# Rewriting the order table of a fused gated-attention and MLP kernel on one Trainium2 core

## The chip, the core and the metric

The kernel runs on one core of a Trainium2 chip (trn2). Its time is the device time of that core in microseconds (us); several runs are taken and their median is compared. The engines are TensorE (PE: matmuls, and beside them its weight loads, PEld), VectorE (DVE), ScalarE (ACT), GpSimd (POOL) and SyncE (SP, which here issues nearly all DMAs).

## The reference

Two parts, the second fed by the first. In float32, with 4 batches, 8 heads, 768 tokens, head size 48:

```python
f = 1.0 / (1.0 + np.exp(-f_logit))
for t in range(S):                                # 768 tokens
    state = f[:, :, t, :, None] * state + k_t (x) v_t     # per head, 48 x 48
    y[:, :, t] = q_t @ state
x = y.transpose(0, 2, 1, 3).reshape(3072, 384)
h = x @ w_in                                      # 384 x 2048
g = h * np.clip(h + 3.0, 0.0, 6.0) / 6.0
out = g @ w_out                                   # 2048 x 384
```

## The kernel before

**Units.** The attention runs in chunks: 24 units of 128 tokens (chunk 0 of the four batches is units 0 to 3, chunk 1 units 4 to 7, and so on). A unit takes these steps, each called by a token name and the unit's number. SP loads `load` (the gates' logits, L308, two buffers), `loadq` (q and k, L312, a ring of three) and `loadv` (v, L317, a ring of three). `gate` is the sigmoid on ACT (L321). DVE makes running products of the gates: `back` (a scan, L327), `rend` (L343 and L344) and `fwd` (a second scan, L347). `kmul` (L340), `qmul` (L353) and `decay` (L356) scale k, q and the carried state; they run on DVE, or on GpSimd if the list ON_POOL names them. TensorE then does `tk` (transposes of k, L411), `kv` (the new state, L430), `att` (the products of q and k, L392, 32 small matmuls), `qs` (q times the old state, L461) and `av` (L478). Between them `ktok` (ACT, L418) copies the transposed k, `mask` (DVE, L399) applies the causal mask to what `att` left in PSUM, `carry0` and `carry1` (L443 to L452) update the state, `xh` (ACT, L497) and `xl` (DVE, L500) write the result as a float16 high and low part, and `hole` (SP, two DMAs at L507) copies some rows of it.

**Weights.** Both weight matrices come in 16 blocks of 128 of the 2048 hidden columns. Block f is loaded by `ld` (SP, `raw`, 768 KB, two buffers, L233) and turned into a float16 high and low part by `z` (ACT, L238), `cy` (ACT, L247), `mid`, `lim`, `dif`, `top` (DVE, L251, L257, L263, L267), `high` (ACT, L272) and `low` or its halves `lowi` and `lowo` (L275, DVE or GpSimd).

**MLP.** The tokens form six groups of 512, one for each chunk. A step is one group with one block; steps are numbered 16 times the group plus the block, 0 to 95. A step is `mm1` (9 float16 matmuls of 128x512, L526), `relu` (ACT, L536), `g` (DVE, L540), `gh` (ACT, L545), `gl` (DVE or GpSimd, L550 and L555) and `mm2` (9 matmuls, L572). For blocks 0 to 4 of group 0 the first matrix product is done in halves of 256 tokens as soon as two units are there: `mm1a`/`mm1b` (L593), `relua`/`relub` (L602), `ga`/`gb` (L606), `mm2a`/`mm2b` (float32, L611); blocks 5 to 7 use `mm2x` (L583). In the last group `mm2` is split into `mm2m0`, `mm2m1` (L572) and the halves `mm2p`, `mm2q` (L626). `outv` (DVE) or `outs` (ACT) reads a finished bank and `od`, `odh` write it out; in the tail `outh` does half of one.

**The checks.** `wtop`, `xtop`, `xsum`, `xleast`, `flag0`, `finite`, `count` and last `judge` (DVE, L725 to L728) reduce the inputs' sizes to one flag. At the end all five engines load the flag and branch (L820) past a general version of the kernel that is not needed for these inputs.

**Warm-ups.** `warm.N` puts N bf16 matmuls of 128x512 on a blank tile (L794) into TensorE's row; nothing reads them.

**What sets the order.** The table ORDER is one long string of tokens `op.number`, with PSUM banks behind a second dot where a step needs them. The program emits the steps in this sequence and ties every instruction to the one before it on its engine, so each engine, and SP's DMA queue, works strictly in the table's order, and waits whenever its next instruction isn't ready. There is no scheduler behind it. A step may change engines only between DVE and GpSimd, by the list ON_POOL, or by its name (`outv`/`outs`). The loop that emits the steps follows.

Of the kernel before, what the change touches and what calls it, by code (L numbers as in the profile page):

```python
# [58 lines left out]
loadv.3 kv.3.0 carry0.3 warm.1 qs.3.2 av.3 loadq.4 carry1.3 xh.2 ld.2 top.1 high.1 mm2a.0 kmul.4 rend.4 xl.2 xh.3 xl.3
lowi.1 fwd.4 mm1a.1.4 z.2 cy.2 mid.2 carry1.2 tk.4.0 ktok.4 qmul.4 lim.2 load.5 relua.1 loadv.4 kv.4.2 ga.1 gate.5  # L60
ld.3 z.3 att.4.2 hole.2 mm2a.1 hole.3 dif.2 top.2 back.5 cy.3 mid.3 loadq.5 kmul.5 decay.4 carry0.4 high.2 mm1b.0.0
relub.0 gb.0 mm1b.1.4 tk.5.1 lowi.2 mm1b.2.0 relub.1 gb.1 lim.3 rend.5 mm1a.2.4 relub.2 mm2b.0 dif.3 fwd.5 top.3 gb.2
mm2b.1 relua.2 loadv.5 ld.4 load.6 ga.2 ld.5 z.4 cy.4 loadq.6 load.7 mm2b.2 carry1.4 mid.4 decay.5 high.3 lim.4 gate.6
lowi.3 mm1a.3.4 dif.4 back.6 top.4 z.5 ktok.5 relua.3 mm1b.3.0 relub.3 high.4 ga.3 kmul.6 mm2a.2 qmul.5 lowi.4 gb.3
mask.4 rend.6 cy.5 mid.5 fwd.6 mm2a.3 lim.5 mm1a.4.0 relua.4 ga.4 ld.6 mm1b.4.4 z.6 gate.7 dif.5 mm2b.3 tk.6.0 ktok.6
relub.4 mm2a.4 loadv.6 qmul.6 top.5 back.7 cy.6 mid.6 att.5.0 qs.4.2 high.5 decay.6 kv.6.0 load.8 gate.8 lowi.5 av.4
xh.4 gb.4 ld.7 mm1.5.4 carry0.6 carry1.6 lim.6 dif.6 loadq.7 mm2b.4 z.7 xl.4 top.6 kv.5.2 relu.5 ld.8 g.5 mm2x.5
mask.5 cy.7 kmul.7 mid.7 loadv.7 tk.7.0 carry0.5 lim.7 hole.4 rend.7 dif.7 high.6 lowi.6 mm1.6.4 z.8 top.7 cy.8 qs.5.2
# [875 lines left out]
```

## Time and profile before

| | |
|---|---|
| median of three runs (489.01, 490.39, 491.16) | 490.39 us |
| the profiled execution | 489.08 us |
| its span in the trace | 487.4 us |
| its mean granted TensorE clock | 0.982 |
| busy PE / weight loads | 464.9 / 248.0 us |
| busy DVE / ACT / POOL | 305.5 / 201.8 / 99.2 us |
| moved by DMA | 40.78 MB, 84 GB/s |
| of it by the instruction queue q8 | 41 transfers, 0.67 MB |

How to read it: the span is the time from the first to the last record; 1.7 us lie outside of it. In a timeline each row is a run of like instructions: its start in us, the time it was busy, the engine, the line, output and inputs, the shape, and how many; in brackets the idle time of the engine ahead of it and what ended that ("issue" means that the engine waited for nothing that the profile shows). In a table of stretches each row has the stretch and its length, the busy time and count of PE, PEld, DVE, ACT and POOL, the clock that TensorE was granted (1.00 is full speed), the share of the 16 DMA engines and the GB/s. In groups of instructions the busy sum and the mean in ns of one come first, then the idle time ahead of them. In the DMA rows stand the count, the size of one and the median time from issue to landing.

### The profile page before, as it was taken

To read this page: it belongs to the slowest core of one execution; us is meant where nothing else is said; L and a number is where in the kernel's file an instruction comes from. 1 tells how busy PE (TensorE), PEld (TensorE's weight loads), DVE (VectorE), ACT (ScalarE), POOL (GpSimd) and SP (SyncE) were. 2 spreads that over 40 slices of the span, in tenths; PEclk is the share of its full clock that TensorE was granted. 3 is DMA by queue.
4 is the path that set the end of the run, shared out by engine and by line. 5 is a ranking of instruction groups with operands and counts; after the bars stand their busy time and mean duration, and the time that the engine had idled before them with its cause. 6 is when DMAs were issued, how large, how long until landed. Compare 5 with 4: busy or idle time off the path is not lost.

```text
span 487.4 us, 11581 instructions
## 1 busy us (share of the span) xinstructions
PE 464.9 (95%) x4980; PEld 248.0 (51%) x4980; DVE 305.5 (63%) x519; ACT 201.8 (41%) x336; POOL 99.2 (20%) x97
## 2 busy tenths in 40 slices
...
GB/s 230 132 294 113 233 171 232 152 152 208 22 93 1 81 50 132 2 196 22 1 66 9 76 77 1 83 152 139 37 43 1 0 1 4 67 0 1 0 1 71
DMA packets 24553, 40.78 MB, mean 84 GB/s; under 512 B 2480, under 2 KB 17072, under 8 KB 24496
## 3 DMA queue, kind: packets, MB, share of 16 engines
...
q8 instruction: 41, 0.67, 0.6%
...
## 4 chain that ended last, share of the span: by engine, by line
PE 77%; DVE 11%; DMA 5%; issue 3%; ACT 2%; POOL 0%; SPq 0%; DVEq 0%; POOLq 0%; ACTq 0%
PE o L572 30%; PE pair L526 22%; PE single L526 9%; DMA qkf<-qk 3%; PE pair L392 2%; PE pair L461 2%; PE o L611 2%; PE pair L478 2%; PE pair L430 2%; DVE tg L540 2%; DMA raw<-w 1%; DVE weight L275 1%; PE single L626 1%; PE pair L626 1%; DVE suffix L327 1%
## 5 line engine op out<-in xcount | busy, mean ns | idle before, releaser
L572 PE MATMUL o<-gg,weight 128*128 128x512 f16 x744 | 170.8, 379 | 3.4 <-ACT gg L545 3.1
L526 PE MATMUL pair<-xts,weight 128*128 128x512 f16 x585 | 133.6, 379 | 0.0
L526 PEld LDWEIGHTS <-weight 128*128 128x128 f16 x819 | 79.0, 98 | 94.4 <-issue 1.6
L572 PEld LDWEIGHTS <-weight 128*128 128x128 f16 x744 | 71.7, 98 | 87.1 <-issue 5.6
L545 ACT ACTIVATE gg<-tg 128x512 f16<-128x512 f32 x88 | 55.0, 628 | 82.2 <-DVE tg L540 50.4
L555 POOL TENSOR_TENSOR gg<-tg,gg 128x512 f16<-128x512 f32 x38 | 47.6, 1254 | 172.0 <-ACT gg L545 157.8
L540 DVE SCALAR_TENSOR_TENSOR tg<-tg,pair 128x512 f32<-128x512 f32 x65 | 43.8, 682 | 53.2 <-ACT tg L536 53.2
L536 ACT ACTIVATE tg<-pair,half 128x512 f32<-128x512 f32 x65 | 44.2, 683 | 77.5 <-PE pair L526 68.7
L526 PE MATMUL single<-xts,weight 128*128 128x512 f16 x234 | 54.8, 379 | 0.0
L555 DVE TENSOR_TENSOR gg<-tg,gg 128x512 f16<-128x512 f32 x34 | 24.7, 731 | 28.7 <-ACT gg L545 28.3
L540 DVE SCALAR_TENSOR_TENSOR tg<-tg,single 128x512 f32<-128x512 f32 x26 | 17.7, 682 | 24.2 <-ACT tg L536 23.0
L347 DVE TENSOR_TENSOR_SCAN suffix<-gates,rend 112x516 f32<-112x516 f32 x24 | 30.5, 1270 | 3.1 <-POOL qkf L340 2.2
L327 DVE TENSOR_TENSOR_SCAN suffix<-gates,unit 112x516 f32<-112x516 f32 x24 | 29.4, 1223 | 2.9 <-ACT gates L321 2.8
L399 DVE TENSOR_TENSOR a<-pair,causal 128x512 f32<-128x512 f32 x24 | 16.4, 684 | 17.7 <-PE pair L478 10.0
L536 ACT ACTIVATE tg<-single,half 128x512 f32<-128x512 f32 x26 | 17.7, 682 | 22.6 <-PE single L526 22.2
L340 POOL TENSOR_TENSOR qkf<-qkf,suffix 112x512 f32<-112x512 f32 x13 | 16.4, 1264 | 48.4 <-DVE suffix L327 34.5
L500 DVE SCALAR_TENSOR_TENSOR xts<-pair,xts 112x512 f16<-112x512 f32 x24 | 16.4, 685 | 12.9 <-ACT xts L497 12.5
L353 POOL TENSOR_TENSOR qkf<-qkf,suffix 112x512 f32<-112x512 f32 x11 | 15.0, 1361 | 44.0 <-PE pair L392 27.3
L497 ACT ACTIVATE xts<-pair 112x512 f16<-112x512 f32 x24 | 14.2, 593 | 21.5 <-PE pair L478 19.0
L392 PE MATMUL pair<-qkf 48*64 48x64 f32 x768 | 17.2, 223 | 5.7 <-issue 5.6
L275 POOL TENSOR_TENSOR weight<-whole,weight 128x384 f16<-128x384 f32 (+1 forms) x10 | 10.6, 1059 | 39.4 <-ACT weight L272 39.4
L392 PEld LDWEIGHTS pair<-qkf 48*64 48x64 f32 x768 | 14.3, 136 | 7.5 <-issue 6.3
...
## 6 DMA issues: line engine op xcount, KB each, us to landing
raw<-w SPq DMA_DIRECT2D x16, 768.0 KB, 4.9
qkf<-qk SPq DMA_DIRECT2D x24, 448.0 KB, 4.6
gates<-fg SPq DMA_DIRECT2D x24, 226.2 KB, 3.2
v<-v SPq DMA_DIRECT2D x24, 200.0 KB, 4.3
...
```

The lines of the kernel that those rows point to most:

```text
L327: nc.vector.tensor_tensor_scan(flat(sf)[:, ::-1], gt[:, 1:][:, ::-1], flat(unit)[:, ::-1], 0.0, op0=ALU.mult, op1=ALU.add,)
L340: engine("kmul", i).tensor_tensor(parts_of(t, 1), parts_of(t, 1), split(sf[:, :, 1:C + 1]), op=ALU.mult)
L347: nc.vector.tensor_tensor_scan(flat(sf), gt[:, :NP * (C + 1)], flat(rend), 0.0, op0=ALU.mult, op1=ALU.add,)
L392: nc.tensor.matmul(d["at"][HC * odd:HC * (odd + 1), e, 2 * n + c], t[rs, 1, n, c, odd], t[rs, 0, n, c, odd], start=True, stop=True,)
L399: nc.vector.tensor_tensor(d["a"].rearrange("r p e t -> r e p t"), d["at"], causal.unsqueeze(1).unsqueeze(1).broadcast_to([128, 2, NP, HC]) ...
L500: nc.vector.scalar_tensor_tensor(parts(1), d["y"][:PR], 2.0 ** XBITS, parts(0), op0=ALU.mult, op1=ALU.subtract)
L526: nc.tensor.matmul(h, win[:, f, a, k * 128:(k + 1) * 128], g["xt"][:, k, :g["n"] // C, b], start=i == 0, stop=i == 3 * KT - 1,)
L536: nc.scalar.activation(d["t"], d["h"], AF.Relu, bias=half, scale=RISE)
L540: nc.vector.scalar_tensor_tensor(d["t"], d["t"], TOP, d["h"], op0=ALU.min, op1=ALU.mult)
L545: nc.scalar.activation(d["gg"][:, 0], d["t"], AF.Copy)
L555: engine("gl", int(g["name"]) * NF + f).tensor_tensor(d["gg"][:, 1], d["t"], d["gg"][:, 0], op=ALU.subtract)
L572: nc.tensor.matmul(g["o"][m], wout[:, f, a, m * 128:(m + 1) * 128], g[f]["gg"][:, b], start=f == 0 and i == 0, stop=f == NF - 1 and i == 2 ...
```

## The change

The string ORDER is written anew: the same steps, 1389 tokens for 1386, in another sequence from the first line to the last. Apart from that:

- ON_POOL has 77 names for 82. kmul.13, kmul.18, qmul.11, gl.17, gl.19, gl.21, gl.35, gl.52, gl.64, gl.67, gl.69 and lowo.4 go from GpSimd to DVE; decay.14, decay.16, qmul.10, gl.45, gl.72, gl.74 and lowo.2 go from DVE to GpSimd. Of the output copies outv.2 becomes outs.2, outv.14 becomes outs.14, and outs.4 becomes outv.4.
- The warm-ups at the start are 16, 2, 3, 4, 4, 3, 5, 6, 2, 2, 1 matmuls; before they were 16, 2, 3, 2, 2, 6, 12, 3, 2, 1. That is 48 for 49.
- The branch at the end carries a hint for the engines' instruction fetch. Before, it named DVE, ACT, POOL and SP at mm1.94 and PE at mm2m1.95. Now it names ACT behind mm1.92 and PE ahead of mm2m1.95, and the other three no longer.
- In the tail `judge` stands behind outv.16, before it stood ahead of mm2p.94; in the list of late steps gl.81 now stands ahead of mm2p.81 and mm2q.81, and mm2.79 and mm1.82 stand between mm1.81 and them.

The diff, with a piece of the table and the code:

```diff
 ORDER = """
...
-mask.0 av.0 xh.0 ld.1 fwd.1 load.3 qmul.1 warm.2 kv.1.2 carry0.1 att.1.0 back.2 mask.1 rend.2 xl.0 z.0 cy.0 mid.0
...
+gate.2 qmul.1 back.2 ktok.1 ld.0 loadq.2 load.3 xh.0 cy.0 xl.0 rend.2 att.1.0 mask.1 warm.4 kv.1.2 z.0 mid.0 carry0.1
...
@@ -781,10 +781,7 @@
-    HINTS = {"mm1.94.2": [e for e in ORDERED if e != ENG.PE], "mm2m1.95": [ENG.PE]}
     for token in ORDER:
-        if token in HINTS:
-            tc.mark_branch_hint_location("general", "LikelyTaken", HINTS[token])
         settle()
         op, i, *tail = token.split(".")
         i = int(i)
@@ -795,6 +792,8 @@
+        elif op == "hint":
+            tc.mark_branch_hint_location("general", "LikelyTaken", [(ENG.PE, ENG.Activation)[i]])
         elif op in FLAG:
```

Three places of the order are needed below. Numbers behind an underscore only number the tiles. The first is SP's queue at the start, from the load of unit 2's q and k on: `gates` is a `load`, `qkf` a `loadq`, `v` a `loadv`, `raw` an `ld`, `xts` a `hole`. Before:

```order
L312 DMA qkf2_227<-qk 112x1024
L233 DMA raw1_256<-w 128x3072
L308 DMA gates1_77<-fg 112x517
L507 DMA xts_112<-xts_112 16x3x256 x4
L312 DMA qkf3_389<-qk 112x1024
L317 DMA v2_393<-v 128x400
L308 DMA gates0_75<-fg 112x517
L317 DMA v3_509<-v 128x400
L312 DMA qkf4_562<-qk 112x1024
L233 DMA raw2_566<-w 128x3072
```

And now:

```order
L312 DMA qkf2_260<-qk 112x1024
L308 DMA gates1_77<-fg 112x517
L317 DMA v2_351<-v 128x400
L233 DMA raw1_353<-w 128x3072
L312 DMA qkf3_357<-qk 112x1024
L507 DMA xts_112<-xts_112 16x3x256 x4
L317 DMA v3_454<-v 128x400
L308 DMA gates0_75<-fg 112x517
L312 DMA qkf4_512<-qk 112x1024
L233 DMA raw2_539<-w 128x3072
L317 DMA v4_541<-v 128x400
```

raw1 (ld.1) stood two places ahead of the rows copy and of unit 3's q and k; now gates1 of unit 3 and v2 stand ahead of it, and a `gates` load can go only when its buffer has been read by `fwd` of two units before. gates0, qkf4, raw2 and v4 now follow each other directly.

The second is DVE from `back` of unit 2 (L327) on; L399 is mask.1, the two rows of L500 are xl.0 (from pair1) and xl.1 (from pair0), L343 and L344 are rend.2, L347 is fwd.2, and L251 to L267 convert weight block 0. Before:

```order
L327 SCALAR_TENSOR_TENSOR suffix0_76<-gates0_75,unit_94 112x516
L399 TENSOR_TENSOR a1_305<-pair0_70,causal_84 128x2x4x64
L343 TENSOR_SCALAR ends_111<-suffix0_76 112x4
L344 RECIPROCAL rend_109<-ends_111 112x4
L500 SCALAR_TENSOR_TENSOR xts_112<-pair1_71,xts_112 112x4x128
L251 TENSOR_SCALAR raw0_225<-top0_311 128x768
L340 TENSOR_TENSOR qkf2_227<-qkf2_227,suffix0_76 112x512
L257 TENSOR_SCALAR top0_311<-top0_311 128x768
L500 SCALAR_TENSOR_TENSOR xts_112<-pair0_70,xts_112 112x4x128
L263 TENSOR_TENSOR top0_311<-top0_311,raw0_225 128x768
L267 SCALAR_TENSOR_TENSOR whole_73<-top0_311,whole_73 128x768
```

And now:

```order
L327 SCALAR_TENSOR_TENSOR suffix0_76<-gates0_75,unit_94 112x516
L500 SCALAR_TENSOR_TENSOR xts_112<-pair1_71,xts_112 112x4x128
L343 TENSOR_SCALAR ends_111<-suffix0_76 112x4
L344 RECIPROCAL rend_109<-ends_111 112x4
L399 TENSOR_TENSOR a1_285<-pair0_70,causal_84 128x2x4x64
L251 TENSOR_SCALAR raw0_258<-top0_264 128x768
L340 TENSOR_TENSOR qkf2_260<-qkf2_260,suffix0_76 112x512
L257 TENSOR_SCALAR top0_264<-top0_264 128x768
L347 SCALAR_TENSOR_TENSOR suffix0_76<-gates0_75,rend_109 112x516
L263 TENSOR_TENSOR top0_264<-top0_264,raw0_258 128x768
L500 SCALAR_TENSOR_TENSOR xts_112<-pair0_70,xts_112 112x4x128
L267 SCALAR_TENSOR_TENSOR whole_73<-top0_264,whole_73 128x768
```

mask.1 went from the place right behind `back` to behind rend.2, xl.0 from behind rend.2 to ahead of it, and fwd.2 and lim to dif of the weight block stand ahead of xl.1 now.

The third is TensorE around att.1 (L392). L430 is kv.1, L794 (in the new file L791) is a warm-up, L478 is av. Before, the last rows of kv.1 and then att.1:

```order
L430 MATMUL pair1_71<-v1_191,ktok1_234 64x48
L430 MATMUL pair1_71<-v1_191,ktok1_234 48x48
L392 MATMUL pair0_70<-qkf1_187 64x64 x16
L794 LDWEIGHTS blank_88
L794 MATMUL idle_124<-blank_88 128x512
```

And now, the end of av.0 and then att.1:

```order
L478 MATMUL pair1_71<-a0_218,v0_159 64x64 x8
L478 MATMUL pair1_71<-a0_218,v0_159 48x64 x8
L392 MATMUL pair0_70<-qkf1_189 64x64 x16
L791 LDWEIGHTS blank_88
L791 MATMUL idle_124<-blank_88 128x512
```

att.1 stood behind all of kv.1; now it comes right behind av.0 (and the four warm-ups and kv.1 come behind att.1). Further on, the table has mm1a.0 (nine matmuls of 128x256), kv.2, att.2, att.3 before, and now att.2, kv.2, mm1a.0, att.3.

More of the change, by code (lines that the diff above doesn't have):

```diff
@@ L59 @@
[L59 to L68, printed above, removed]
@@ L134 @@
[L134 to L138 removed]
+load.0 loadq.0 gate.0 load.1 back.0 rend.0 kmul.0 gate.1 warm.16 tk.0.1 ktok.0 fwd.0 back.1 loadv.0 warm.2 kv.0.2
```

169 lines of the change are left out of this document (89 added, 80 removed).

## Prediction

> **What bounds the kernel now.** I read the page's head first, then busy time by stage, then the timelines of TensorE (PE) and VectorE (DVE) over the first 62 us, the DMA view of short stretches, and the tail.
>
> ```profile
> span 487.4 us, 11581 instructions
> PE 464.9 (95%) x4980; PEld 248.0 (51%) x4980; DVE 305.5 (63%) x519; ACT 201.8 (41%) x336; POOL 99.2 (20%) x97
> q8 instruction: 41, 0.67, 0.6%
> 61.00:122.00 61.00, 58.38 (x765) 32.50 (x764) 58.91 (x100) 40.48 (x59) 15.15 (x13) 1.00 0.57 183
> 122.00:474.00 352.00, 349.54 (x3420) 177.90 (x3419) 198.30 (x324) 129.60 (x222) 76.33 (x64) 1.00 0.17 47
> ```
>
> The last two rows are stages: after the length, the busy time of PE, weight loads, DVE, ACT and POOL. From 122 to 474 us PE is busy 349.5 of 352 us. It is the bound; its matmuls are the same in both kernels, so an order can save only its 2.5 us of gaps there. From 61 to 122 us DVE is busy 58.9 of 61 us and PE 58.4: both are full. What an order can win lies before 61 us. PE there:
>
> ```profile
> 12.12 0.60 PE L794 MATMUL idle<-blank 128*128 128x512 bf16 x2
> 12.91 0.85 PE L430 MATMUL pair<-v,ktok 64*64 64x48 f32 x46 [0.18 <-ACT xts L497]
> 17.22 0.90 PE L392 MATMUL pair<-qkf 48*64 48x64 f32 x19 [3.16 <-issue]
> 35.41 0.46 PE L392 MATMUL pair<-qkf 48*64 48x64 f32 x16 [2.42 <-issue]
> 38.87 2.93 PE L611 MATMUL o<-th,whole 128*128 128x256 f32 x6
> 41.59 2.00 PE L593 MATMUL single<-xts,weight 128*128 128x256 f16 x9
> 45.69 1.56 PE L611 MATMUL o<-th,whole 128*128 128x256 f32 x6
> 47.09 1.15 PE L593 MATMUL pair<-xts,weight 128*128 128x256 f16 x9
> ```
>
> Twice PE stops inside a block of attention matmuls and waits for nothing that the profile shows ("issue"): 3.16 us in att.1, 2.42 us in att.3. DVE works on unit after unit in a fixed order, and its largest waits answer to these:
>
> ```profile
> 12.62 0.69 DVE L353 TENSOR_TENSOR qkf<-qkf,suffix 112x512 f32<-112x512 f32 x1
> 18.16 0.69 DVE L399 TENSOR_TENSOR a<-pair,causal 128x512 f32<-128x512 f32 x1 [3.70 <-PE pair L392]
> 21.64 0.69 DVE L500 SCALAR_TENSOR_TENSOR xts<-pair,xts 112x512 f16<-112x512 f32 x1 [0.79 <-ACT xts L497]
> 35.94 0.69 DVE L399 TENSOR_TENSOR a<-pair,causal 128x512 f32<-128x512 f32 x1 [2.78 <-PE pair L392]
> 44.95 0.42 DVE L606 SCALAR_TENSOR_TENSOR th<-th,single 128x256 f32<-128x256 f32 x1 [2.36 <-ACT th L602]
> ```
>
> mask.1 waits 3.70 us for att.1, mask.3 2.78 us for att.3, ga.1 2.36 us for relua.1 behind mm1a.1. What PE waits for is its instructions. Here is the count between the two stops, and then the one line that matters from the DMA view of four stretches (10.3 to 14.6, 14.6 to 15.9, 29.2 to 32.7, 32.7 to 34.0 us):
>
> ```profile
> 17.20:35.38 18.18, 14.33 (x253) 8.75 (x252) 13.52 (x24) 6.01 (x11) 1.36 (x1) 0.84 0.63 185
> q1 hardware_dynamic: 310, 1.46, 97.9%
> q8 instruction: 1, 0.02, 5.3%
> q1 hardware_dynamic: 246, 1.15, 103.0%
> q8 instruction: 1, 0.02, 5.2%
> ```
>
> 253 matmuls, each with its weight load, and a few waits are about 512 instructions. The 41 instruction transfers stand against PE's 9,960 matmuls and weight loads, so one transfer brings about 256; the stops lie two transfers apart. While the loads' queue q1 fills the engines (97.9%, 103%) no instruction moves; each fetch runs only in the stretch behind, and PE resumes 1.3 to 1.4 us after that stretch. Counting back 256 instructions, the block that ended at the first stop was entered in att.0 at about 10.2 us: 7.0 us from entry to resumption. The second was entered in kv.2 at about 29.2: 6.2 us. A block on which PE works longer than that never stops it. Now the clock, by stretches of 3.41 us (PE busy, granted clock, DMA share, GB/s):
>
> ```profile
> 12.60:16.02 3.42, 1.28 (x62) 1.00 1.02 333
> 16.02:19.43 3.41, 2.21 (x37) 0.50 0.21 58
> 33.08:36.50 3.42, 1.09 (x65) 1.00 0.97 327
> 36.50:39.91 3.41, 3.32 (x54) 0.50 0.03 10
> 108.18:111.59 3.41, 1.51 (x7) 1.00 0.14 34
> ```
>
> A stop leaves a stretch with 1.1 to 1.3 us of work, and half clock follows; a stretch with 1.51 us kept the full clock. The second spell hits mm2a.0 and mm1a.1: 2.93 and 2.00 us against 1.56 and 1.15 at full clock, 2.2 us together.
>
> **The change part by part.** It computes the same, with one warm-up matmul less.
>
> A. *First stop.* att.1 moves ahead of four warm-ups and kv.1, so the boundary falls near the middle of kv.1. Two more prices:
>
> ```profile
> L392 PE MATMUL pair<-qkf 48*64 48x64 f32 x768 | 17.2, 223 | 5.7 <-issue 5.6
> raw<-w SPq DMA_DIRECT2D x16, 768.0 KB, 4.9
> qkf<-qk SPq DMA_DIRECT2D x24, 448.0 KB, 4.6
> gates<-fg SPq DMA_DIRECT2D x24, 226.2 KB, 3.2
> v<-v SPq DMA_DIRECT2D x24, 200.0 KB, 4.3
> ```
>
> att.1 waits for qmul.1, which ends on DVE at 13.31 (12.62 plus 0.69). An att takes 0.7 us (17.2 over 24 of them), four warm-ups 0.9 to 1.2, half of kv.1 0.4: PE reaches the boundary at about 15.4, 5.2 us after entry. On SP's queue raw.1 now stands behind gates.3, which waits for fwd.1. So gates.2, raw.0 and qkf.2, 1.44 MB, are queued ahead of the fetch, not 2.2 MB. At the 340 GB/s of the first stretch (1.46 MB in 4.3 us) that is 2.2 us less: a latency of 4.8. No stop then; at the old latency one of 1.8. mask.1 finds att.1 done when back.2 ends, and xl.0, now ahead of it, needs xh.0, done by about 14. I take the whole 3.7 us, and leave the 0.79 us of xl.1 in.
>
> B. *Second stop.* mm1a.0 (1.0 us) and most of kv.2 now lie inside the block, whose PE work was 3.0 us and becomes 4.2, with about 0.9 of waits: 5.1 us. At its entry gates.4, qkf.4 and part of raw.2 are queued, 0.9 to 1.5 MB against 2.3 MB. Latency between 4.5 and 6.2: no stop, or one of 1.1. Of the 2.78 us I take 2.0.
>
> C. *Clock.* Stops under 1.9 us leave every stretch over 1.5 us of work, so no half clock: 2.2 of the 2.36 us. In the page "TensorE: Matmul & The Clock Gate" (section on HAM oscillation) the Trainium skill gives the rule that only gaps over about 3.4 us must be avoided. The trace differs: gaps of 3.16 and 2.42 us were followed by a clock of 0.50. By the rule C would not hang on the stops, and the sum below would be 2.2 us smaller.
>
> A to C: 7.9 us, all as DVE time before 46 us. DVE is full from 61 us and PE from 122, so the lead is carried to the end. Two waits behind stay as they are, their order on DVE, ACT and SP being almost the same:
>
> ```profile
> 58.33 0.89 ACT L238 ACTIVATE whole<-raw 128x768 int32<-128x768 uint32 x1 [2.85 <-DMA raw<-w]
> 107.82 0.95 DVE L257 TENSOR_SCALAR top<-top 128x768 int16<-128x768 int16 x1
> 110.08 1.24 PE L572 MATMUL o<-gg,weight 128*128 128x512 f16 x5 [2.58 <-ACT gg L545]
> ```
>
> D. *GpSimd.* lim.13 (107.82) ran beside lowo.6 on GpSimd, ahead of PE's 2.58 us wait; lowo.6 moves behind low.15, but lowo.2 joins GpSimd's run in front. Between 0.95 won and as much lost; I take 0.4 won. Of the other moves between DVE and GpSimd none lies where DVE is full: nothing, and up to 0.6 us each if that cover is gone.
>
> E. *Late gaps.*
>
> ```profile
> 426.20 0.27 PE L626 MATMUL pair<-gg,weight 128*128 128x256 f16 x1 [1.35 <-DVE gg L550]
> SPq L820 <- SPq L820: 3.4, 3, 2.9
> ```
>
> mm2q.81 waits 1.35 us for gl.81, which DVE runs after gl.82. In the new order it runs before, and mm2.79 and mm1.82 lie between: that goes. New gaps are possible up to the 2.5 us of the old order; net 0.7 won.
>
> F. *Tail.* judge moves behind outv.16, about 0.4 us later against PE's end, and SP branches after it. SP's branch waits 2.9 us (last row) although SP was named in the old hint, so not naming it costs nothing; GpSimd and DVE reach their branch earlier and are covered by SP's wait. Half of the 0.4 lies beside the landing of the last output: 0.2 lost, at worst 2.9.
>
> **Sum.** 7.9 + 0.4 + 0.7 - 0.2 = 8.8 us. The profiled execution took 489.08 us, so 480.3. The median of the three runs, 490.39, stands 1.31 above it: 481.6 on that scale.
>
> **The rivals.** *Shorter stops* (22%): the fetches keep their 7.0 and 6.2 us. Then PE stops for 1.8 us in kv.1, of which DVE feels 1.5 at xl.1, and 1.1 in att.3, and one of the stretches falls to the half clock (1.1 of C): 3.7 us less, 485.3. For it: part of the loads in front of both fetches stays. Against: 2.2 and 0.9 us less of them.
>
> *Loads hold DVE* (8%): started earlier, the weights cannot come earlier, and the ACT wait of 2.85 for raw grows by the 4 us that the 61 us stretch cannot give: 485.6. Against: the DMA share is 0.57 there.
>
> *Slower* (6%): gates.4, qkf.4, raw.2 and v.4, now issued together, stand ahead of the second fetch, and the DMA of unit 2 and 3 ahead of the first. From a latency of 10 us on, PE stops 4.8 and 4.9 us: A and B turn into losses of 1.1 and 2.1, and a third spell of half clock (3.41 of 6.83 us) takes C back and 1.2 more; with D to F, 3.5 us slower: 493.9. Against: 10 us asks for 3.4 MB in front of the fetch, and at most 1.8 are there.
>
> *The stops do not answer to the order* (6%): then A to C fall away, and 0.9 us remain: 489.5. The Trainium skill speaks for this in "Runtime: NRT & Kernel Launch", section Instruction fetch mechanics: crossing a block of 256 instructions is mostly hidden. The trace disagrees, with two stops of 3.16 and 2.42 us, 512 instructions apart.
>
> **How the numbers follow.** The forecast, 481.6, has 58%, and with B between 1.7 and 2.8, D, E and F at their ends, runs from 478 to 484.5. The first two rivals, both faster, bring the range to 486; below, 477.5 if the loads' earlier start also removes small DVE waits. The last two, 12%, stay out. Within 0.5% is 2.45 us, about what a measurement of this kernel can tell from no change. Faster: 58 + 22 + 8 = 88%; same 6%; slower 6%.
>
> **What would show it.** Right: no "issue" wait over 1 us on PE before 45 us, granted clock 1.00 in every stretch from 9 to 60 us, mm2a.0 starting at 30 to 33 us (38.87 before), mask.1 and mask.3 without waits over 1 us, PE's 2.58 us wait kept but some 8 us earlier, and none at mm2q.81. Wrong: an "issue" wait of 2 us or more in kv.1, att.3 or later, a stretch at 0.50 behind it, or a wait for raw that grows by what the start has won.

## The result, and the profile after

The changed kernel takes 477.38 us (median of four runs, 474.87 to 478.42) against 490.77 of the kernel before (489.01 to 491.17): a ratio of 0.9726, 95% interval 0.9681 to 0.9772. That is 13.4 us less; 8.8 were forecast, and 477.38 lies 0.12 us below the range. Two further sets of runs of the same kernel gave medians of 475.30 (0.9726, 0.9691 to 0.9760) and 475.41 (0.9753, 0.9717 to 0.9789).

The profiled execution is the longest of the first four, 478.42 us. Its page begins:

```profile
span 476.5 us, 11577 instructions
PE 460.4 (97%) x4979; PEld 246.2 (52%) x4979; DVE 305.0 (64%) x522; ACT 202.7 (43%) x338; POOL 89.0 (19%) x92
```

TensorE at the start, and behind it the wait at mm2.11, in its timeline:

```profile
13.16 0.69 PE L392 MATMUL pair<-qkf 48*64 48x64 f32 x32
16.11 0.56 PE L430 MATMUL pair<-v,ktok 64*48 64x48 f32 x25 [0.67 <-issue]
30.67 1.56 PE L611 MATMUL o<-th,whole 128*128 128x256 f32 x6
35.33 0.60 PE L593 MATMUL single<-xts,weight 128*128 128x256 f16 x4 [2.17 <-issue]
37.54 2.56 PE L611 MATMUL o<-th,whole 128*128 128x256 f32 x6
101.24 2.24 PE L572 MATMUL o<-gg,weight 128*128 128x512 f16 x9 [1.65 <-ACT gg L545]
```

att.1 (13.16) runs through. The first stop has become 0.67 us in the middle of kv.1, att.3 has none, and mm2a.0 starts at 30.67, 8.2 us earlier. A new stop of 2.17 us stands in mm1a.1, at the boundary behind the one in att.3. mask.1 and mask.3 no longer wait, on VectorE's timeline:

```profile
15.04 0.66 DVE L399 TENSOR_TENSOR a<-pair,causal 128x512 f32<-128x512 f32 x1
28.39 0.69 DVE L399 TENSOR_TENSOR a<-pair,causal 128x512 f32<-128x512 f32 x1
```

The clock behind the new stop, in stretches of 3.41 us (TensorE busy, granted clock, DMA share, GB/s): a stretch with 1.24 us of work, and then half clock. The stretches are laid so that one begins where the half clock does; in each profile all spells of half clock before 120 us lie a whole number of 3.41 us apart.

```profile
32.77:36.18 3.41, 1.24 (x31) 1.00 0.35 109
36.18:39.59 3.41, 3.41 (x62) 0.50 0.73 215
```

The second set's profile (475.35 us, near its median) shows the same kernel without that spell:

```profile
16.71 0.56 PE L430 MATMUL pair<-v,ktok 64*48 64x48 f32 x25 [1.25 <-issue]
34.41 0.60 PE L593 MATMUL single<-xts,weight 128*128 128x256 f16 x4 [0.93 <-issue]
36.03 1.56 PE L611 MATMUL o<-th,whole 128*128 128x256 f32 x6
98.69 2.25 PE L572 MATMUL o<-gg,weight 128*128 128x512 f16 x9 [1.65 <-ACT gg L545]
410.68 0.49 PE L626 MATMUL pair<-gg,weight 128*128 128x256 f16 x3
466.66 1.15 PE L626 MATMUL single<-gg,weight 128*128 128x256 f16 x9
```

Its mean granted clock is 0.998, for 0.993 in the first. Held against the rows of before, it leads by 9.7 us at mm2a.1 (36.03 for 45.69), by 11.4 at mm2.11 (98.69 for 110.08), and mm2q.81 (410.68) has no wait for gl.81; TensorE ends at 467.81, where the last row of before is this:

```profile
480.44 1.15 PE L626 MATMUL pair<-gg,weight 128*128 128x256 f16 x9
```

That is 481.59, so 13.8 us at TensorE's end and 14.1 in the spans (473.3 for 487.4).

### The profile page after: what moved, and what is told of

Read it like the earlier page. It is cut to its first block, busy times and chain, and to the rows that moved or that the text cites. A ratio compares the mean times of both kernels' runs of the same rounds, so it can differ in the third digit from the quotient of the medians.

```text
span 476.5 us, 11577 instructions
## 1 busy us (share of the span) xinstructions
PE 460.4 (97%) x4979; PEld 246.2 (52%) x4979; DVE 305.0 (64%) x522; ACT 202.7 (43%) x338; POOL 89.0 (19%) x92
## 4 chain that ended last, share of the span: by engine, by line
PE 85%; DVE 5%; DMA 4%; issue 2%; ACT 2%; POOL 0%; SPq 0%; POOLq 0%; ACTq 0%; DVEq 0%
PE o L572 31%; PE pair L526 25%; PE single L526 12%; PE pair L461 2%; PE pair L392 2%; PE pair L478 2%; PE o L611 2%; DMA qkf<-qk 2%; PE o L583 2%; PE pair L430 2%; DMA raw<-w 1%; PE single L626 1%; PE pair L626 1%; PE single L593 1%; DVE suffix L347 1%
## 5 line engine op out<-in xcount | busy, mean ns | idle before, releaser
L526 PE MATMUL pair<-xts,weight 128*128 128x512 f16 x558 | 127.5, 379 | 0.1
L540 DVE SCALAR_TENSOR_TENSOR tg<-tg,pair 128x512 f32<-128x512 f32 x62 | 42.1, 682 | 72.4 <-ACT tg L536 72.3
L536 ACT ACTIVATE tg<-pair,half 128x512 f32<-128x512 f32 x62 | 42.0, 683 | 73.8 <-PE pair L526 70.3
L555 POOL TENSOR_TENSOR gg<-tg,gg 128x512 f16<-128x512 f32 x33 | 40.1, 1220 | 164.0 <-ACT gg L545 163.8
L526 PE MATMUL single<-xts,weight 128*128 128x512 f16 x261 | 61.2, 380 | 0.0
L555 DVE TENSOR_TENSOR gg<-tg,gg 128x512 f16<-128x512 f32 x39 | 27.0, 691 | 20.1 <-ACT gg L545 19.9
L536 ACT ACTIVATE tg<-single,half 128x512 f32<-128x512 f32 x29 | 19.8, 684 | 37.0 <-PE single L526 29.7
L327 DVE TENSOR_TENSOR_SCAN suffix<-gates,unit 112x516 f32<-112x516 f32 x24 | 30.0, 1249 | 8.1 <-ACT gates L321 8.1
L347 DVE TENSOR_TENSOR_SCAN suffix<-gates,rend 112x516 f32<-112x516 f32 x24 | 29.9, 1248 | 3.0 <-POOL qkf L340 2.8
L540 DVE SCALAR_TENSOR_TENSOR tg<-tg,single 128x512 f32<-128x512 f32 x29 | 19.8, 681 | 16.9 <-ACT tg L536 16.9
L353 POOL TENSOR_TENSOR qkf<-qkf,suffix 112x512 f32<-112x512 f32 x11 | 15.1, 1372 | 47.5 <-DVE suffix L347 47.5
L340 POOL TENSOR_TENSOR qkf<-qkf,suffix 112x512 f32<-112x512 f32 x11 | 13.9, 1268 | 32.7 <-DVE suffix L327 20.1
L500 DVE SCALAR_TENSOR_TENSOR xts<-pair,xts 112x512 f16<-112x512 f32 x24 | 16.4, 682 | 5.3 <-ACT xts L497 5.3
L321 ACT ACTIVATE gates<-gates 112x512 f32<-112x512 f32 x24 | 14.9, 623 | 7.2 <-DMA gates<-fg 6.1
L399 DVE TENSOR_TENSOR a<-pair,causal 128x512 f32<-128x512 f32 x24 | 16.3, 679 | 2.2 <-PE pair L392 1.2
L392 PE MATMUL pair<-qkf 48*64 48x64 f32 x768 | 17.0, 224 | 0.5 <-ACT ktok L418 0.4
```

The costliest lines, as they stand in the source:

```text
L327: nc.vector.tensor_tensor_scan(flat(sf)[:, ::-1], gt[:, 1:][:, ::-1], flat(unit)[:, ::-1], 0.0, op0=ALU.mult, op1=ALU.add,)
L347: nc.vector.tensor_tensor_scan(flat(sf), gt[:, :NP * (C + 1)], flat(rend), 0.0, op0=ALU.mult, op1=ALU.add,)
L353: engine("qmul", i).tensor_tensor(parts_of(t, 0), parts_of(t, 0), split(sf[:, :, 1:]), op=ALU.mult)
L392: nc.tensor.matmul(d["at"][HC * odd:HC * (odd + 1), e, 2 * n + c], t[rs, 1, n, c, odd], t[rs, 0, n, c, odd], start=True, stop=True,)
L399: nc.vector.tensor_tensor(d["a"].rearrange("r p e t -> r e p t"), d["at"], causal.unsqueeze(1).unsqueeze(1).broadcast_to([128, 2, NP, HC]) ...
L500: nc.vector.scalar_tensor_tensor(parts(1), d["y"][:PR], 2.0 ** XBITS, parts(0), op0=ALU.mult, op1=ALU.subtract)
```

## The experiments

Ratios are to the kernel before, run beside each. On them one us is 0.2%. TensorE's stream of matmuls, weight loads and waits is fetched in blocks of 256; by the records of the traces a block ends at the 193rd of them and at every 256th from there, which in the changed kernel's first profile are 16.11, 22.86, 27.88, 35.33 us and so on. The prediction's two stops lie at the first and the third of these boundaries. Where an expectation gives the time a fetch takes to start, it is counted from TensorE's entry into the block ahead of the one that is fetched to the transfer of the instruction queue that brings it. A lead in a trace is held against the one profile of the kernel before. Two other profiles with the same first 124 steps pass mm1.5 at 65.21 and 63.57 us, that one at 68.96, so a lead that includes the start can be too long by 4 to 5 us.

**The start against the rest.** The tables agree on the set of the first 124 steps, up to kv.4, so each half can be had alone.

```diff
-load.0 loadq.0 load.1 gate.0 back.0 rend.0 kmul.0 fwd.0 warm.16 tk.0.1 loadv.0 gate.1 back.1 ktok.0 warm.2 kv.0.0
...
+load.0 loadq.0 gate.0 load.1 back.0 rend.0 kmul.0 gate.1 warm.16 tk.0.1 ktok.0 fwd.0 back.1 loadv.0 warm.2 kv.0.2
...
+xl.2 high.1 xh.3 cy.2 z.2 lowi.1 xl.3 tk.4.0 fwd.4 mid.2 qmul.4 mm1a.1.4 ktok.4 lim.2 relua.1 kv.4.2 load.5 ga.1
```

> The kernel before, with only its first 124 steps (everything up to kv.4, the same steps in both kernels) in the new order. Theory: the gain of the start, 7.2 us in the traces at mm1b.1, belongs to these steps, and so do the 2.7 us by which the medians differ more than the two profiled executions do (stops of TensorE that vary from one execution to the next): ratio 0.978 to 0.985, no stop in att.1 or att.3, a stop in mm1a.1 in some executions. Rival: the start wins little by itself, since the stages behind it (DVE full from 61 us) give the lead back when they keep the old order: ratio 0.992 or more.

Measured: 0.9834 (0.9792 to 0.9877), so 8.1 us. On the trace its lead was 10.9 us at mm1.5; then it lost 1.3 at mm2x.6 and 1.4 at mm2.11. This is TensorE at mm1a.1 and at mm2.11:

```profile
34.28 0.60 PE L593 MATMUL single<-xts,weight 128*128 128x256 f16 x4 [1.73 <-issue]
100.48 3.59 PE L572 MATMUL o<-gg,weight 128*128 128x512 f16 x9 [2.59 <-ACT gg L545]
```

The wait at mm2.11 is that of before, but the nine matmuls behind it took 3.59 us and not 2.24. The other half is the changed kernel with its lines up to kv.4 replaced by the old ones:

```diff
-carry0.0 qmul.0 loadq.1 carry1.0 kmul.1 warm.3 att.0.0 rend.1 fwd.1 loadv.1 load.2 mask.0 tk.1.4 qs.0.2 warm.4 av.0
...
+loadq.1 carry0.0 carry1.0 loadv.1 qmul.0 warm.3 att.0.0 qs.0.2 load.2 gate.2 rend.1 ld.0 loadq.2 kmul.1 tk.1.4 ktok.1
...
+lowi.1 fwd.4 mm1a.1.4 z.2 cy.2 mid.2 carry1.2 tk.4.0 ktok.4 qmul.4 lim.2 load.5 relua.1 loadv.4 kv.4.2 ga.1 dif.2
```

> The changed kernel with its first 124 steps in the old order, the rest new. Theory: the two stops of 3.2 and 2.4 us and the two spells of half clock are back, and what is left is the wait at mm2.11 (0.9), the wait at mm2q.81 and xsum.3 behind it (1.9) and the tail: 2.5 to 3.3 us, ratio 0.993 to 0.995. Rival: the later stages hold more than the traces show, the 2.7 us of the medians included: ratio 0.990 or less.

Measured: 0.9910 (0.9874 to 0.9945), 4.4 us. That lies between the theory and the rival, and the interval reaches into both. Either way the late stages hold more than I had given them: the 0.9 us of D to F would be 0.998, outside the interval. The halves add up to 12.5 of the 13.4.

**The late wait alone.**

```diff
-mm1.81.2 od.12 relu.81 mm2m0.80 outv.13 mm1.82.0 mm1.83.1 g.81 gh.81 relu.82 g.82 gh.82 gl.82 gl.81 mm2q.81 mm2p.81
+mm1.81.2 od.12 relu.81 mm2m0.80 outv.13 mm1.82.0 mm1.83.1 g.81 gh.81 gl.81 relu.82 g.82 gh.82 gl.82 mm2q.81 mm2p.81
```

> The kernel before, with gl.81 alone moved ahead of g.82 (DVE). Theory: the 1.35 us wait of TensorE at mm2q.81 goes and nothing takes its place: 1.3 to 1.5 us less in the trace from there on, ratio 0.997. Rival: the wait goes over to the next steps (g.82 starts later, mm2q.82 waits): no difference behind mm1.84.

Measured: 0.9962 (0.9937 to 0.9987). In the trace mm2q.81 starts without a wait (it waited 1.35 us) and nothing behind it waits instead: the lead grows by 1.5 us between mm1.80 and mm1.84 and stays.

```profile
421.95 0.49 PE L626 MATMUL pair<-gg,weight 128*128 128x256 f16 x3
422.27 0.49 PE L626 MATMUL single<-gg,weight 128*128 128x256 f16 x3
```

**The changed kernel again.** No edit.

> The changed kernel as it is, once more, beside the others on one chip. Theory: its executions differ by whether TensorE stops in mm1a.1 (2.2 us and a stretch at half clock in the first profile, 478.42 us): the times lie between 474 and 479, the granted clock is 0.997 in the short ones and 0.993 in the long ones, and a profile of a short one has no such stop. Rival: the spread lies elsewhere and the stop is there in each: a short execution with the same stop.

Measured: 0.9726, with times from 474.20 to 476.81 us; the rows are above. The rival was right. The stop in mm1a.1 is there in all three profiles of this kernel, 2.17, 0.93 and 1.59 us; what the long one has besides is the spell of half clock, which only the 2.17 brought.

**The first stop by its two causes.** Spacing: TensorE's row near unit 1.

```diff
-mask.0 av.0 xh.0 ld.1 fwd.1 load.3 qmul.1 warm.2 kv.1.2 carry0.1 att.1.0 back.2 mask.1 rend.2 xl.0 z.0 cy.0 mid.0
+mask.0 warm.4 av.0 xh.0 ld.1 fwd.1 load.3 qmul.1 att.1.0 warm.4 kv.1.2 carry0.1 back.2 mask.1 rend.2 xl.0 z.0 cy.0 mid.0
```

> The kernel before with TensorE's row alone altered near unit 1: four warm-ups ahead of av.0, and att.1 with four warm-ups (for two) ahead of kv.1; DVE and SP keep their order. Theory (TensorE waits for its next 256 instructions): the block of the first stop gets 4.1 us of work for 3.0, the stop stays at the same place in the count, which is now the middle of kv.1, and is 1.1 us shorter (0.8 to 2.0 us); att.1 runs through, mask.1 waits less than 1 us; the second stop (att.3) is as before; ratio 0.992 to 0.997. Rival: the stop belongs to att.1 itself (something it waits for that the profile doesn't show): att.1 then stops 2 us or more in its new place, ratio 0.998 to 1.002.

Loads: raw.1 behind load.3.

```diff
-mask.0 av.0 xh.0 ld.1 fwd.1 load.3 qmul.1 warm.2 kv.1.2 carry0.1 att.1.0 back.2 mask.1 rend.2 xl.0 z.0 cy.0 mid.0
+mask.0 av.0 xh.0 fwd.1 load.3 ld.1 qmul.1 warm.2 kv.1.2 carry0.1 att.1.0 back.2 mask.1 rend.2 xl.0 z.0 cy.0 mid.0
```

> The kernel before with SP's queue alone altered: the load raw.1 goes behind load.3, which waits for fwd.1, so 0.77 MB less is queued ahead of the first instruction fetch. Theory: that fetch starts 1.0 to 2.0 us earlier after TensorE enters its block (3.4 to 4.5 us before) and the stop in att.1 is shorter by as much, 0.5 to 1.5 us; mask.1 waits as much less; ratio 0.994 to 0.998. Rival: the time that a fetch takes doesn't depend on the loads ahead of it: a stop of 2.2 to 3.2 us as before, ratio 1.000.

Both edits:

```diff
-mask.0 av.0 xh.0 ld.1 fwd.1 load.3 qmul.1 warm.2 kv.1.2 carry0.1 att.1.0 back.2 mask.1 rend.2 xl.0 z.0 cy.0 mid.0
+mask.0 warm.4 av.0 xh.0 fwd.1 load.3 ld.1 qmul.1 att.1.0 warm.4 kv.1.2 carry0.1 back.2 mask.1 rend.2 xl.0 z.0 cy.0 mid.0
```

> The two edits together (TensorE's row near unit 1, raw.1 behind load.3), all else as before. Theory: no stop over 0.5 us before 20 us, no stretch at half clock before 30 us, mask.1 without a wait over 1 us, and the lead at mm1a.0 3 to 5 us; the second stop in att.3 stays and its spell of half clock too; ratio 0.988 to 0.993. Rival: the lead is lost at the second stop (what comes earlier waits there longer): ratio 0.996 or more.

And the undoing, in the changed kernel:

```diff
-gate.2 qmul.1 back.2 ktok.1 ld.0 loadq.2 load.3 xh.0 cy.0 xl.0 rend.2 att.1.0 mask.1 warm.4 kv.1.2 z.0 mid.0 carry0.1
-warm.3 qs.1.0 av.1 xh.1 gate.3 kmul.2 lim.0 fwd.2 loadv.2 ld.1 carry1.1 dif.0 loadq.3 xl.1 top.0 high.0 warm.5 tk.2.2
+gate.2 qmul.1 back.2 ktok.1 ld.0 loadq.2 ld.1 load.3 xh.0 cy.0 xl.0 rend.2 att.1.0 mask.1 warm.4 kv.1.2 z.0 mid.0 carry0.1
+warm.3 qs.1.0 av.1 xh.1 gate.3 kmul.2 lim.0 fwd.2 loadv.2 carry1.1 dif.0 loadq.3 xl.1 top.0 high.0 warm.5 tk.2.2
```

> The changed kernel with raw.1 alone put back to its old place in SP's queue, ahead of load.3 and the loads behind it. Theory: the first fetch has 0.77 MB more ahead of it, starts 1 us later, and the stop in kv.1 grows from 0.7 to 1.3 us to 1.7 to 2.3; gates.3 and v.2 land later too; 1 to 2 us slower than the changed kernel. Rival: spaced as the instructions now are, the order of the loads no longer matters: no difference.

The first stop in the four kernels, on TensorE's timelines: spacing alone, loads alone, both, and raw.1 put back.

```profile
16.70 0.56 PE L430 MATMUL pair<-v,ktok 64*48 64x48 f32 x25 [1.33 <-issue]
```

```profile
15.74 0.90 PE L392 MATMUL pair<-qkf 48*64 48x64 f32 x19 [1.84 <-issue]
```

```profile
15.62 0.56 PE L430 MATMUL pair<-v,ktok 64*48 64x48 f32 x25 [0.21 <-issue]
26.30 0.85 PE L430 MATMUL pair<-v,ktok 64*64 64x48 f32 x46 [1.39 <-DMA v<-v]
32.69 0.51 PE L392 MATMUL pair<-qkf 48*64 48x64 f32 x19 [2.32 <-issue]
```

```profile
16.61 0.56 PE L430 MATMUL pair<-v,ktok 64*48 64x48 f32 x25 [1.49 <-issue]
```

With the records of the instruction queue beside them (times in us; "old" and "new" as in the two kernels). The second and third line are the profiles of the next kernels with the old start, the one with gl.81 alone and the one with the new rest:

```
spacing loads   block entered  fetch starts  TensorE goes on  stop
old     old         10.24         14.70           17.22       3.16   the kernel before
old     old         10.52         14.21           16.73       2.38   gl.81 alone
old     old         10.14         13.57           16.24       2.27   the new rest
old     new         10.08         13.19           15.74       1.84
new     old         10.08         14.32           16.69       1.33
new     new         10.12         13.20           15.61       0.21
new     old          9.80         14.08           16.61       1.49   raw.1 put back
```

With raw.1 in front of it the fetch starts 3.4 to 4.5 us after the entry in the six profiles that have it there, without it 2.7 to 3.5 in the eleven others: 0.8 us less on the mean, with an overlap. Spacing leaves that alone; TensorE then reaches the boundary 5.3 us after the entry and not 3.8, and that shortens the stop. The stop moved from att.1 into kv.1, to the place in the count where the block ends, so it isn't att's. That much is as in the theory. The sizes are less sure than the two forecasts that they met, since the same old start gave stops of 3.16, 2.38 and 2.27 us. The times are not as in the theory: 1.0022 (0.9995 to 1.0049) for the spacing, 0.9986 (0.9956 to 1.0017) for the loads, 0.9974 (0.9943 to 1.0004) for both, where the rival had 0.996 or more. (The profiled execution of the loads' kernel, 491.28 us, was its longest, so only the first stop and the clock behind it are read from it.) The lead of the pair is 3.0 us at mm1a.0; the rows show where it shrinks, at kv.2, which waits 1.39 us for v.2, and at the second stop, 2.32 us, there as before. With raw.1 put back the stop is 1.49 us, less than the 1.7 to 2.3 of the theory, and the time 0.9770 (0.9729 to 0.9811) for 0.9753 of the changed kernel beside it, too close to tell apart.

**Who holds the start's gain.** TensorE's row alone in the new order up to kv.4, and the complement. In the first kernel carry1.2 stands behind tk.3, which writes the same bank, so the carried state of unit 2 isn't the reference's; the instructions are as many.

```diff
-loadq.1 carry0.0 carry1.0 loadv.1 qmul.0 warm.3 att.0.0 qs.0.2 load.2 gate.2 rend.1 ld.0 loadq.2 kmul.1 tk.1.4 ktok.1
...
+xh.3 z.2 cy.2 carry1.2 lowi.1 xl.3 tk.4.0 fwd.4 mid.2 qmul.4 mm1a.1.4 ktok.4 lim.2 relua.1 load.5 loadv.4 kv.4.2 ga.1
```

> The kernel before, with TensorE's row alone in the new order up to kv.4 (its warm-ups too); VectorE, ScalarE and SP keep their old order there, and all is old behind. Theory: spacing and loads each hold a part of the start's gain. With old loads the first fetch starts 3.4 to 4.5 us after the block is entered and the second as late; with 4.1 and 4.2 us of work in the two blocks both stops shrink by about 1.1 us (0.8 to 2.0 and 0.9 to 1.3 left), neither leaves a half clock, and mask.1 and mask.3 wait under 1 us: 3 to 5 us of the 8.1 of the whole start, ratio 0.990 to 0.994. Rival: TensorE's row holds nearly all of it: ratio 0.985 or less. Second rival: without the other rows it holds nothing: 0.998 or more.

```diff
-loadq.1 carry0.0 carry1.0 loadv.1 qmul.0 warm.3 att.0.0 qs.0.2 load.2 gate.2 rend.1 ld.0 loadq.2 kmul.1 tk.1.4 ktok.1
...
+high.1 xh.3 cy.2 z.2 lowi.1 xl.3 fwd.4 mid.2 mm1a.1.4 tk.4.0 qmul.4 ktok.4 lim.2 relua.1 kv.4.2 load.5 ga.1 gate.5
```

> The complement: VectorE, ScalarE and SP in the new order up to kv.4, TensorE's row old there (att.1 behind kv.1, mm1a.0 ahead of kv.2), and all old behind. Theory: the first fetch starts at 3.1 to 3.4 us, but the block has only 3.0 us of work: a stop of 1.5 to 2.0 us in att.1 and one of about 2 us in att.3, for which mask.1 and mask.3 wait; 1 to 4 us of the 8.1, ratio 0.992 to 0.998. Rival: the order of the loads and of VectorE holds nearly all: ratio 0.985 or less.

Measured: 1.0009 (0.9978 to 1.0039) and 0.9984 (0.9954 to 1.0015). Neither half is worth anything that can be told from nothing; together they are worth 8.1 us. TensorE's timeline with its own row alone (and qmul.2 on VectorE, L353), and then with the others' rows alone:

```profile
16.14 0.56 PE L430 MATMUL pair<-v,ktok 64*64 64x48 f32 x23 [0.93 <-DVE xts L500]
17.06 0.56 PE L430 MATMUL pair<-v,ktok 64*48 64x48 f32 x25 [0.36 <-issue]
26.44 0.69 PE L392 MATMUL pair<-qkf 48*64 48x64 f32 x32 [3.86 <-ACT whole L238]
25.63 0.67 DVE L353 TENSOR_TENSOR qkf<-qkf,suffix 112x512 f32<-112x512 f32 x1
```

```profile
14.70 0.85 PE L430 MATMUL pair<-v,ktok 64*64 64x48 f32 x46 [1.10 <-DVE xts L500]
16.01 0.56 PE L392 MATMUL pair<-qkf 48*64 48x64 f32 x19 [0.15 <-issue]
32.00 0.46 PE L392 MATMUL pair<-qkf 48*64 48x64 f32 x16 [2.14 <-issue]
```

In the first the big stops are gone, but att.2, which now comes early, waits 3.86 us, and kv.1 for xl.0. The view puts att.2's wait down to ScalarE's z.1, but att.2 reads what qmul.2 writes, and that ends at 26.30, behind back.3 in VectorE's old row. In the second kv.1 waits 1.10 us for xl.0, so only 0.15 us is left of the stop in att.1 (1.5 to 2.0 were forecast), and the second stop is there, 2.14 us. The second rival of the first kernel holds; the theory of the second is just missed.

**Half clock at mm2.11.** The start's kernel (first experiment) with eight idle matmuls in the wait:

```diff
+        elif op == "heat":
+            for _ in range(i):
+                nc.tensor.matmul(
+                    single.rearrange("p (a n) -> p a n", n=128), blank,
+                    blank.unsqueeze(1).broadcast_to([128, 4, 128]), start=True, stop=True,
+                )
...
-mm1.12.0 g.11 xh.7 gh.11 dif.13 lowo.3 ld.14 top.13 high.13 decay.8 relu.12 gl.11 mm2.11 z.14 hole.5 cy.14 carry0.8
+mm1.12.0 g.11 xh.7 gh.11 dif.13 lowo.3 ld.14 top.13 high.13 decay.8 relu.12 gl.11 heat.8 mm2.11 z.14 hole.5 cy.14 carry0.8
```

> The kernel with the new start and the old rest, and eight idle matmuls (1.7 us, on a bank that is free there) in front of mm2.11, inside the 2.6 us that TensorE waits there anyway. Theory: mm2.11 took 3.59 us without them because the wait leaves a stretch with too little work and half clock follows; with them the stretch stays full, mm2.11 takes 2.24 us, 1.3 us less than that kernel: ratio to before 0.979 to 0.982 (0.9834 without). Rival: the half clock there doesn't come from TensorE's idle time: mm2.11 takes 3.5 us with them too.

Measured: 0.9842 (0.9800 to 0.9883), no different from 0.9834 and above the forecast of 0.979 to 0.982; 1.3 us, 0.3%, is less than this interval can tell. In the trace the matmuls behind the wait are back at 2.24 us:

```profile
96.43 1.89 PE L800 MATMUL single<-blank 128*128 128x512 bf16 x8
99.20 2.24 PE L572 MATMUL o<-gg,weight 128*128 128x512 f16 x9 [0.88 <-ACT gg L545]
```

The spell does not come each time, so one profile without it proves little by itself. The tally of all profiles says more: with the old order at this place the wait was 2.57 to 2.60 us and mm2.11 took 2.24, 3.59, 3.57, 2.24, 3.62, 3.18, 3.71 and 2.25 us; with the new order the wait was 1.65 to 1.67 and mm2.11 took 2.24 or 2.25 in all eight. Two stretches of 3.41 us around the wait in the start's kernel, and one in the second profile of the changed kernel, each laid on that profile's own spells of half clock:

```profile
96.72:100.13 3.41, 1.17 (x6) 1.00 0.13 46
100.13:103.54 3.41, 3.06 (x8) 0.50 0.59 209
```

```profile
95.81:99.22 3.41, 1.76 (x9) 1.00 0.18 63
```

How much of the wait falls into one stretch differs from execution to execution. In the five profiles with the spell the stretch that ends at it had 0.8 to 1.2 us of work, in the three without it 1.5 us or more. A wait of 1.65 us leaves at least 1.76 of 3.41 us, and the eight profiles had 1.76 to 2.24.

**The hints.** The changed kernel with the old ones.

```diff
+    HINTS = {"mm1.94.2": [e for e in ORDERED if e != ENG.PE], "mm2m1.95": [ENG.PE]}
     for token in ORDER:
+        if token in HINTS:
+            tc.mark_branch_hint_location("general", "LikelyTaken", HINTS[token])
...
-mm1.91.0 gh.90 gl.90 mm2p.90 relu.91 g.91 gh.91 mm2q.90 mm2m1.90 mm2m0.90 gl.91 mm1.92.1 hint.1 mm2q.91 relu.92
+mm1.91.0 gh.90 gl.90 mm2p.90 relu.91 g.91 gh.91 mm2q.90 mm2m1.90 mm2m0.90 gl.91 mm1.92.1 mm2q.91 relu.92
...
-xleast.5 flag0.0 mm2m0.94 mm2m0.95 mm2m1.94 hint.0 mm2m1.95 mm2q.93 outs.15 mm2q.94 finite.0 count.0.0 outv.16 od.15
+xleast.5 flag0.0 mm2m0.94 mm2m0.95 mm2m1.94 mm2m1.95 mm2q.93 outs.15 mm2q.94 finite.0 count.0.0 outv.16 od.15
```

> The changed kernel with the old hints for the branch at the end (DVE, ACT, POOL and SP at mm1.94, TensorE at mm2m1.95). Theory: SP waits about 3 us at its branch with and without a hint, so nothing changes: within 0.3 us of the changed kernel, 5.3 to 5.9 us from TensorE's last matmul to the end of the span. Rival: the hints that were dropped cost instruction transfers or time in the tail: 0.5 to 1 us slower than the changed kernel.

> The changed kernel once more, to stand beside the three others on one chip: 474 to 479 us, ratio to before 0.969 to 0.977.

Measured: 0.9766 (0.9722 to 0.9811) with the old hints, 0.9753 (0.9717 to 0.9789) without. SP's wait at its branch (in us in all, how often, the longest), with the old hints and with the new:

```profile
SPq L822 <- SPq L822: 3.5, 1, 3.5
```

```profile
SPq L819 <- SPq L819: 3.1, 1, 3.1
```

From TensorE's end to the end of the span it is 5.9 us with the old hints in the new order and 5.7 to 5.9 in the kernels with the old rest; the profiles of kernels with the new ones show 5.4 to 6.2. No effect can be told.

**Two tries for a faster kernel.** The stop in mm1a.1 has loads in front of its fetch, and three of them could be issued earlier. The changed kernel with all three, and then with two, moved ahead:

```diff
-ktok.2 hole.0 qmul.2 hole.1 z.1 warm.6 att.2.2 cy.1 back.3 kv.2.0 carry0.2 carry1.2 lowi.0 warm.2 mm1a.0.4 rend.3
+ktok.2 loadv.3 load.4 loadq.4 hole.0 qmul.2 hole.1 z.1 warm.6 att.2.2 cy.1 back.3 kv.2.0 carry0.2 carry1.2 lowi.0 warm.2 mm1a.0.4 rend.3
```

> The changed kernel with three loads of SP (loadv.3, load.4, loadq.4: 0.87 MB) put ahead of hole.0, so that they are issued from 15 to 19 us, where the DMA engines stand nearly idle (0.12 from 19.6 to 23.0 us), and not from 21.9 to 23.4. Theory: a fetch waits only for what is queued ahead of it; then the fourth fetch (its block is entered at about 28 us, 3.4 to 4.8 us until it starts) has less in front of it, starts within 3 us, and the stop in mm1a.1 never comes: 0 to 1.5 us faster than the changed kernel. Rival: a fetch waits until the loads' queue runs dry, whenever they were issued; then the second fetch (entered at 16 us, needed at 23) starts later than 21 us and TensorE stops in kv.2 for 1 to 2 us: slower by as much.

```diff
-ktok.2 hole.0 qmul.2 hole.1 z.1 warm.6 att.2.2 cy.1 back.3 kv.2.0 carry0.2 carry1.2 lowi.0 warm.2 mm1a.0.4 rend.3
+ktok.2 loadv.3 load.4 hole.0 qmul.2 hole.1 z.1 warm.6 att.2.2 cy.1 back.3 kv.2.0 carry0.2 carry1.2 lowi.0 warm.2 mm1a.0.4 rend.3
```

> The changed kernel with loadv.3 and load.4 (0.43 MB) put ahead of hole.0; loadq.4 stays behind hole.1. Theory: half of the relief that three loads gave the fourth fetch (2.4 us for 4.4), without the wait of mm1a.0 for the copied rows, since less stands ahead of them: no stop over 1 us in mm1a.1, 0 to 1 us faster than the changed kernel (ratio to before 0.970 to 0.974). Rival: the rows still come late and mm1a.0 waits over 0.5 us: as slow as with three loads, or slower than the changed kernel.

Measured: 0.9810 (0.9759 to 0.9861) and 0.9756 (0.9709 to 0.9804). In both the stop in mm1a.1 is gone: the fetch starts 2.4 and 1.6 us after its block is entered (3.4 to 4.8 in the changed kernel), and the second fetch comes no later, which speaks for a fetch that waits only for the loads issued ahead of it. It is not shown: the kernel with the idle matmuls, whose loads are not moved, has no stop there in its profile either (1.9 us). And TensorE waits elsewhere, with three loads for the copied rows in mm1a.0, with two in tk.4 for kmul.4, which waits for q and k of unit 4:

```profile
25.92 1.14 PE L593 MATMUL single<-xts,weight 128*128 128x256 f16 x9 [1.33 <-DMA xts<-xts]
```

```profile
39.84 0.60 PE L411 MATMUL pair<-ident,qkf 112*128 112x112 f32 x4 [1.47 <-DVE qkf L340]
```

Neither beats the changed kernel.

## Why the prediction was wrong, step by step

**The step that failed** is the sum of D, E and F, "0.4 + 0.7 - 0.2": 0.9 us, where the rest of the order alone measures 4.4 (2.7 to 6.2). The profiles agree: from mm1.5 to TensorE's end the eight with the new rest take 409.2 to 410.3 us, the nine with the old rest 412.2 to 415.5.

- D took the wait at mm2.11 as 2.58 us that stay but for 0.4. It became 1.65, so 0.9 went, the upper end of D's own range, and by another operation than the one it named. lim.13 takes 0.95 us in both kernels; what became shorter is mid.13 ahead of it, 2.22 us before and 1.35 now:

```profile
105.57 2.22 DVE L251 TENSOR_SCALAR raw<-top 128x768 int16<-128x768 int16 x1
```

```profile
97.59 1.35 DVE L251 TENSOR_SCALAR raw<-top 128x768 int16<-128x768 int16 x1
```

  It is so in all nine profiles with the old rest and all eight with the new. GpSimd's run beside it has one `lowo` less, as D had read; that this is the cause is argued, no run moves it alone. The second part of what D missed, the half clock, I had excluded by one row: a stretch with 1.51 us of work "kept the full clock". That was true of that execution; in five of the eight profiles with the old order here the half clock fell on mm2.11 and lengthened it by 0.9 to 1.5 us, 0.8 on the mean of the eight. With 1.65 us of wait it came in none of eight. That those 0.8 us are in the times too is an estimate, which the idle matmuls could not confirm.
- E found the right wait at mm2q.81 and the right cause, and then took off half for "new gaps" that no row showed. The edit alone gains 1.5 us in the trace. A second wait went that E had not counted, at mm2m0.95 in the tail, for gh.95 (0.27 us, the row below) and gl.95 (0.14); it is in all profiles with the old rest and in none with the new, and mm2m0.94 and mm2m0.95 together take 0.7 us less. New gaps didn't come: from 122 to 464 us TensorE is idle for 1.2 us in the second profile of the changed kernel (second row), for 2.5 in the same stretch before.

```profile
476.96 2.40 PE L572 MATMUL o<-gg,weight 128*128 128x512 f16 x9 [0.27 <-ACT gg L545]
```

```profile
122.00:464.00 342.00, 340.80 (x3353) 173.57 (x3351) 195.34 (x324) 125.00 (x214) 61.52 (x54) 1.00 0.18 50
```
- F expected judge's later place to cost 0.2 us. It cost nothing that shows.

These come to 3.9 us (0.9, 0.8, 1.5 and 0.7). The interval of the 4.4 leaves open what the rest is.

**A to C**, "7.9 us, all as DVE time before 46 us", were right as a sum: the start alone measures 8.1 (6.0 to 10.2). In part that is luck, for the terms were not what the edits are worth one by one. A put the latency from entry to resumption at 4.8 us; it is 5.9 to 6.2 in the three profiles of the changed kernel, and was 7.0, 6.2 and 6.1 with the old start. So a stop of 0.5 to 1.3 us stayed, but in kv.1, where mask.1 doesn't feel it. A was priced at 3.7 us; the two edits that take the first stop away measure 1.3 (-0.2 to 2.8). What limits the start changes hands between fetches, loads and the rows of VectorE and ScalarE, and a price per wait holds only once the next in line is moved as well.

**B** said no stop, or 1.1 us, in att.3, and there is none. It didn't follow the count on to the fourth fetch, where 0.9 to 2.2 us of stop turned up in mm1a.1. In one of the three profiles that is the sign that the prediction had named for being wrong: 2 us or more, and half clock behind it. The rival "shorter stops" came nearest to that in kind, in the wrong block.

**C** held for the changed kernel: its stops under 1.9 us were followed by no half clock, the one of 2.17 us was. C's rule, that over 1.5 us of work in a stretch keep the full clock, did not hold. In the spacing kernel half clock followed the stop of 1.33 us in kv.1, with 2.01 us of work left in the stretch, and in the loads' kernel the one of 1.84 us, with 1.76. At mm2.11, where the matmuls are of 128x512, 1.5 us were enough. What else counts there stays open. The spacing kernel:

```profile
14.99:18.41 3.42, 2.01 (x71) 1.00 0.34 116
18.41:21.82 3.41, 3.41 (x38) 0.50 0.07 19
```

The page "TensorE: Matmul & The Clock Gate" of the Trainium skill (section on HAM oscillation) allows gaps up to about 3.4 us; here single gaps of 1.3 to 3.2 us were at times enough for the half clock.

**Carried to the end** held. With the new rest the lead stayed (11.0 us at mm1.5, 11.4 at mm2.11), and in the kernel with the new start and the idle matmuls too (10.9 at mm1.5, 11.1 at the end). In the start's kernel it went from 10.9 to 8.1, but that is this one execution: 1.3 us went at mm2x.6 by waits (0.70 and 0.28 us) that only one other profile has, and 1.4 by the half clock at mm2.11.

**The wait for raw** behind mm2a.3 (1.72 us on TensorE before) was not in the sum. It was 1.11, 0 and 0 us in the three profiles of the changed kernel and 0 to 2.1 in those with the old rest. With one order it comes and goes, so it is no gain of the change.

**The scale.** The sum was made on one execution and shifted by its distance to a median of three. The old kernel's executions run from 485.57 to 491.03 us in one set of 17, and in its order stops and spells of half clock differ from profile to profile. That makes one execution a poor base, but it does not explain the miss: the gain is 13.3 and 12.8 us in the two further sets as well, for 8.8.
